# Two DFT stages of a fused GFNet and mixture-of-experts kernel: full-array products against quarter-array products of sums and differences

## The chip, the cores and the metric

The kernel runs on one core of one Trainium2 chip. The metric is device time in microseconds, from the first to the last instruction. Engine names follow the profile: PE is TensorE (matmul), PEld its weight loads, DVE is VectorE, ACT is ScalarE, POOL is GpSimd, SP is the engine that issues most transfers.

## The reference: what is computed

Two layers in a row, all in fp32. First a global filter over the sequence: a real FFT of length 2496 per batch and channel, a product with a complex filter, and the inverse. Then a top-1 mixture of experts over the 8 x 2496 = 19968 rows that come out.

```python
# batch 8, seq 2496, dim 256
X = np.fft.rfft(x, axis=1)
Y = X * (filt_r + 1j * filt_i)[None]
y = np.fft.irfft(Y, n=2496, axis=1)             # -> (19968, 256)

logits = y @ w_gate                             # 8 experts
expert_idx = np.argmax(logits, axis=1)
gate_w = softmax(logits)[row, expert_idx]
for e in range(8):                              # rows sorted by expert
    h = np.maximum(x_sorted[lo:hi] @ w1[e], 0)  # 256 -> 1024
    y_sorted[lo:hi] = h @ w2[e]                 # 1024 -> 256
out = gate_w[:, None] * y_sorted[inv_perm]
```

## The kernel before

The FFT is a product of two short DFTs: 2496 = 39 x 64, with q in 0..38 and t in 0..63. Per batch there are four stages of matmuls. Stage one (`stage_a`) takes the DFT over q (39 points, real input, so 20 frequencies f with real and imaginary part, 40 numbers). Stage two (`stage_b`) is the complex DFT over t and the filter. Stage three (`stage_c`) goes back over t. Stage four (`stage_d`) goes back over q. Between the stages the data goes through DRAM (`zd`, `ud`) to change the layout. Then each batch is routed: `turn_y` transposes the rows, `logits` multiplies by the gate, `route` finds each row's place, and rows are scattered into lists by expert, from which the expert matmuls (L796, L837, L854) read.

In stages one and four, three values of t are handled by one matmul through a block-diagonal matrix: 3 x 39 = 117 rows by 3 x 40 = 120 columns. A batch has 22 such groups, in six chunks `CH` of up to four groups (five of 4 and one of 2).

```python
NB, NG = 3, 22
TP, TK = NB * N1, NB * NS            # 117, 120

def bank():                          # one of 7 PSUM banks
    return ps.tile([P, 512], F32, tag="bank", name="bank")

def evac(o, i, n):                   # PSUM to SBUF, on DVE or ACT by a running estimate of both
    either(n, lambda: nc.vector.tensor_copy(o, i), lambda: nc.scalar.copy(out=o, in_=i))

def stage_a(b, c):
    i0, n = CH[c]
    xt = ins.pop(("x", b, c))
    zo = sb.tile([TK, 4, D], F32, tag="st", name="zo", bufs=4)
    for j in range(0, n, 2):
        p = bank()
        mm(p[:TK, :], lhsT=tas, rhs=xt[:TP, j:j + 2, :], start=True, stop=True)          # L342
        evac(zo[:, j:j + 2, :], p[:TK, :].rearrange("p (t d) -> p t d", t=2), 512)
    for r, m, v in columns(zd[b], i0, n):
        move(v, zo[:r, m])           # one transfer per chunk (two for the last)
    ...

def stage_d(b, c):
    ...
    yo = outs["o", b, c] = sb.tile([P, 4, DR], F32, tag="y", name="yo", bufs=YB)[:TP]
    for j in range(0, n, 2):
        p = bank()
        if i0 + j + 2 < NG:
            mm(p[:TP, :], lhsT=tds, rhs=ui[:TK, j:j + 2, :], start=True, stop=True)      # L401
        else:
            for i, k in enumerate((TK, NS)):                                             # L405
                mm(p[:TP, i * D:(i + 1) * D], lhsT=tds[:k, :], rhs=ui[:k, j + i, :], start=True, stop=True)
        evac(yo[:, j:j + 2, :D], p[:TP, :].rearrange("p (i d) -> p i d", i=2), 512)
```

After stage four each chunk is transposed, and the gate is applied. The gate's matmul has 32 output rows, and four of them go side by side to four strips of 32 rows of one PSUM tile:

```python
def turn_y(b, c):
    ...
                nc.tensor.transpose(                                                     # L476
                    pt[:, 2 * i + dh, :TP], yo[:, j + i, dh * P:(dh + 1) * P], ident[:TP, :TP])

def logits(b, g):
    ...
    for dh in range(DH):
        for j in js:                 # up to four
            mm(lt[j * CT:(j + 1) * CT], lhsT=wg[:, dh, :], rhs=pair[j][:, :, dh, :],     # L490
               start=(dh == 0), stop=(dh == DH - 1))
```

Each engine runs its instructions in program order. The program's order comes from a loop that keeps an estimated clock `now`, takes FFT steps from a list of slots (slot k holds stages two and three of batch k, stage one of batch k+1, stage four and routing of batch k-1), and puts expert matmuls of already routed batches in between. After the last FFT step only expert work is left.

```python
steps.append((..., lambda c=c: stage_a(k + 1, c), ("x", k + 1, c), 0.43 * CH[c][1]))     # us on PE, estimated
steps.append((at, lambda c=c: stage_d(k - 1, c), ..., 0.43 * CH[c][1]))
```

A matmul of fp32 stands in the trace as two instructions (two passes), so that one `mm` with a right side of 512 columns is two MATMUL lines.

Of the kernel before, what the change touches and what calls it, by code (L numbers as in the profile page):

```python
# [19 lines left out]
P = 128  # L20
S = 2496
D = 256
# [16 lines left out]

def token(q, t):  # L40
    return (q * N2 * pow(N2, -1, N1) + t * N1 * pow(N1, -1, N2)) % S


def coefficients():

    k = np.arange(S)
    of = np.zeros((N2, N1), int)
    of[k * pow(N1, -1, N2) % N2, k * pow(N2, -1, N1) % N1] = k
    return of[:, :NF]


def dft_tables():

    w = 2.0 * np.pi
    q = np.arange(N1)
    t = np.arange(N2)  # L60

    ta = np.zeros((NB, N1, NB, NS))
    td = np.zeros((NB, NS, NB, N1))
    for f in range(NF):
        ang = w * ((q * f) % N1) / N1
        for j in range(NB):
            ta[j, :, j, f] = np.cos(ang)
            td[j, f, j] = (2.0 if f else 1.0) / S * np.cos(ang)
            if f:
                ta[j, :, j, NF + f] = -np.sin(ang)  # L70
                td[j, NF + f, j] = -2.0 / S * np.sin(ang)

    ang = w * ((t[:, None] * t[None, :]) % N2) / N2
    c, sn = np.cos(ang), np.sin(ang)
    tb = np.block([[c, -sn], [sn, c]])
    tc = np.block([[c, sn], [-sn, c]])

    ids = np.zeros((NB, N1, NG))
    valid = np.zeros((NB, N1, NG))
    for j in range(NB):  # L80
        for i in range(len(range(j, N2, NB))):
            ids[j, :, i] = token(q, NB * i + j)
            valid[j, :, i] = 1.0


    sg = np.where(coefficients() <= S // 2, 1.0, -1.0)

    return {
        "ta": ta.reshape(TP, TK),
        "tb": tb,  # L90
        "tc": tc,
        "td": td.reshape(TK, TP),
        "sg": np.concatenate([sg[:, :NF // 2], sg[:, NF // 2:]]),
        "ids": ids.reshape(TP, NG),
        "valid": valid.reshape(TP, NG),
    }


def lay_x(x):

    out = np.zeros((x.shape[0], P, NG, D), x.dtype)
    q = np.arange(N1)
    for j in range(NB):
        for i in range(len(range(j, N2, NB))):
            out[:, j * N1:(j + 1) * N1, i] = x[:, token(q, NB * i + j)]
    return out
# [12 lines left out]
def kernel(  # L119
# [13 lines left out]
    valid: bass.AP,  # L133
    out: bass.AP,
# [47 lines left out]
    tas = cst.tile([TP, TK], F32, name="tas")  # L182
    tbs = cst.tile([P, P], F32, name="tbs")
    tcs = cst.tile([P, P], F32, name="tcs")
    tds = cst.tile([TK, TP], F32, name="tds")
    sgs = cst.tile([P, NF // 2], F32, name="sgs")
# [5 lines left out]
    tri = cst.tile([TP, TP], F32, name="tri")  # L192
    ones = cst.tile([TP, P], F32, name="ones")
    segs = {w: cst.tile([P, E * w], F32, name=f"seg{w}") for w in (8, NG % 8)}
    ids0 = cst.tile([TP, NG], F32, name="ids0")
    vld = cst.tile([TP, NG], F32, name="vld")
# [63 lines left out]
    def load_rest():  # L260
        nc.sync.dma_start(out=tds, in_=td)
        nc.vector.memset(wg, 0.0)
        nc.sync.dma_start(out=wg[:, :, :E], in_=moe_w_gate.rearrange("(i p) e -> p i e", p=P))
        nc.sync.dma_start(out=ids0, in_=ids)
        nc.sync.dma_start(out=vld, in_=valid)

    def make_constants():
        make_identity(nc, ident)
        nc.gpsimd.memset(ones, 1.0)
        nc.gpsimd.affine_select(  # L270
            out=tri, in_=ones[:, :TP], compare_op=ALU.is_gt, fill=0.0, base=0, pattern=[[1, TP]], channel_multiplier=-1
        )
        for w, seg in segs.items():
            nc.gpsimd.memset(seg, 1.0)
            nc.gpsimd.memset(seg.rearrange("p (e t) -> p e t", t=w)[:, :, 0:1], 0.0)
        nc.gpsimd.memset(cnt, 0.0)
        nc.gpsimd.iota(prow, pattern=[[0, 1]], base=0, channel_multiplier=1)
        nc.gpsimd.iota(tau_i, pattern=[[1, 64]], base=0, channel_multiplier=0)
        nc.vector.tensor_copy(tau0, tau_i)
        nc.gpsimd.iota(e_i, pattern=[[1, E]], base=0, channel_multiplier=0)  # L280
        nc.vector.tensor_scalar(em8, in0=e_i, scalar1=-float(E), scalar2=None, op0=ALU.add)
        nc.vector.tensor_scalar(eoff, in0=e_i, scalar1=float(TE), scalar2=None, op0=ALU.mult)
        nc.vector.memset(done, 0.0)
        nc.vector.memset(one, 1.0)


    def columns(ap, i0, n):
# [4 lines left out]
        if m < n:  # L292
            yield NS, slice(m, n), rows[(NG - 1) * TK:, :].rearrange("(i p) d -> p i d", p=NS)

# [29 lines left out]
    def load_z(b, c):  # L324
        f0, n = FH[c]
        zi = fin(("z", b, c))
        nc.sync.dma_start(out=zi[:HP, :n], in_=zd[b][:, f0:f0 + n, :])
        nc.sync.dma_start(out=zi[HP:, :n], in_=zd[b][:, NF + f0:NF + f0 + n, :])

    def load_u(b, c):  # L330
        i0, n = CH[c]
        ui = fin(("u", b, c))
        for r, m, v in columns(ud[b], i0, n):
            nc.sync.dma_start(out=ui[:r, m], in_=v)

    def stage_a(b, c):
        i0, n = CH[c]
        xt = ins.pop(("x", b, c))
        zo = sb.tile([TK, 4, D], F32, tag="st", name="zo", bufs=4)
        for j in range(0, n, 2):  # L340
            p = bank()
            mm(p[:TK, :], lhsT=tas, rhs=xt[:TP, j:j + 2, :], start=True, stop=True)  # L342
            evac(zo[:, j:j + 2, :], p[:TK, :].rearrange("p (t d) -> p t d", t=2), 512)
# [31 lines left out]
    def stage_c(b, f):  # L375
# [8 lines left out]
        if j == 2:  # L384
            f0 = f - 2
            move(ud[b][:, f0:f0 + 4, :], uo[:HP])
            move(ud[b][:, NF + f0:NF + f0 + 4, :], uo[HP:])
# [3 lines left out]
    def stage_d(b, c):  # L391
        if c == 0:
            lgs[b] = sb.tile([TP, NG, E], F32, tag="lg", name="lg")
# [3 lines left out]
        yo = outs["o", b, c] = sb.tile([P, 4, DR], F32, tag="y", name="yo", bufs=YB)[:TP]  # L397
        for j in range(0, n, 2):
            p = bank()
            if i0 + j + 2 < NG:  # L400
                mm(p[:TP, :], lhsT=tds, rhs=ui[:TK, j:j + 2, :], start=True, stop=True)  # L401
            else:

                for i, k in enumerate((TK, NS)):
                    mm(p[:TP, i * D:(i + 1) * D], lhsT=tds[:k, :], rhs=ui[:k, j + i, :], start=True, stop=True)  # L405
# [6 lines left out]
    def first_a(c):  # L412
# [6 lines left out]
        for j in range(0, n, 2):  # L419
            p = bank()[:, :4 * TK]  # L420
            for h in range(DH):
                for i in range(2):
                    mm(p[:, (2 * h + i) * TK:(2 * h + i + 1) * TK], lhsT=xt[:TP, j + i, h * P:(h + 1) * P], rhs=tas,
# [46 lines left out]
    def turn_y(b, c):  # L470
        yo = outs["o", b, c]
        for j in range(0, CH[c][1], 2):
            pt = bank().rearrange("p (i q) -> p i q", i=4)
            for i in range(2):
                for dh in range(DH):
                    nc.tensor.transpose(  # L476
                        pt[:, 2 * i + dh, :TP], yo[:, j + i, dh * P:(dh + 1) * P], ident[:TP, :TP]
                    )
            yt = yts[b, c, j] = sb.tile([P, 4, TP], F32, tag="yt", name="yt", bufs=4)
            evac(yt, pt[:, :, :TP], 4 * TP)  # L480

    def logits(b, g):
# [4 lines left out]
        lt = psr.tile([P, 2, E * NG], F32, tag="rk", name="lt")[:, :, :TP]  # L487
# [4 lines left out]
        ls = sb.tile([P, 2, TP], F32, tag="ls", name="ls", bufs=1)  # L492
# [3 lines left out]
    def turn_logits(b):  # L496
        g, w, ls = outs.pop(("l", b))
        n = w // CT
        pt = bank()[:TP, :2 * w].rearrange("p (i w) -> p i w", i=2)
# [8 lines left out]
    def route(b, g):  # L508
        t0 = 8 * g
        w = min(8, NG - t0)  # L510
        lg = lgs[b][:, t0:t0 + w]
        sh3 = (TP, w, E)
        she = (TP, E, w)

        def small(name, *shape, dt=F32, tag=None, rows=TP):
# [12 lines left out]
        nc.vector.tensor_tensor(oh, oh, em8[:TP, None, :].to_broadcast(sh3), op=ALU.mult)  # L528
# [4 lines left out]
        nc.vector.tensor_tensor(idx, idx, vld[:, t0:t0 + w], op=ALU.mult)  # L533
# [3 lines left out]
            oe, idx[:, None, :].to_broadcast(she), em8[:TP, :, None].to_broadcast(she), op=ALU.is_equal  # L537
# [10 lines left out]
        mm(rk[:TP, 0, :E * w], lhsT=tri, rhs=oef, start=True, stop=True)  # L548
        mm(rk[:, 1, :E * w], lhsT=ones, rhs=oef, start=True, stop=True)
        rks = sb.tile([P, 2, 8 * E], F32, tag="rks", name="rks", bufs=1)  # L550
        nc.vector.tensor_copy(rks[:TP, 0, :E * w], rk[:TP, 0, :E * w])
# [5 lines left out]
        for c, yo in enumerate(yos):  # L557
            n = min(4, w - 4 * c)
            sh8 = (TP, n, 8)
            nc.vector.tensor_scalar(  # L560
                yo.bitcast(I32)[:, :n, D:D + 8], in0=ids0[:, t0 + 4 * c:t0 + 4 * c + n, None].to_broadcast(sh8),
# [13 lines left out]
        nc.vector.tensor_tensor(posf, runf[:TP], rks[:TP, 1, :E * w], op=ALU.subtract)  # L575
        nc.vector.tensor_tensor(posf, posf, rks[:TP, 0, :E * w], op=ALU.add)
        yield 2
        bs = sb.tile([TP, E], F32, tag="bs", name="bs", bufs=1)
        nc.vector.tensor_tensor(bs, cnt[:TP], eoff[:TP], op=ALU.add)
# [6 lines left out]
        row = sb.tile([TP, 8], U32, tag="row", name="row", bufs=2)[:, :w]  # L586
        nc.vector.tensor_copy(row, rowf)  # L587
# [3 lines left out]
        for t in range(w):  # L591
            m = N1 if t0 + t == NG - 1 else TP
# [9 lines left out]
    def pad_rows():  # L602
# [6 lines left out]
        fill = pools["moe"].tile([P, DR], F32, name="fill", bufs=1)  # L609
# [6 lines left out]
    def scatter(key, at, what):  # L616
# [4 lines left out]
            in_offset=None,  # L621
        )
# [249 lines left out]
    def slot(k):  # L872
# [19 lines left out]
        if k + 1 < B:  # L892
            for c in range(nch):
                steps.append(((0.25 if k == 0 else 0.0) + 0.7 * c / nch, lambda c=c: stage_a(k + 1, c), ("x", k + 1, c), 0.43 * CH[c][1]))
        if k > 0:
            for c in range(nch + 3):
# [3 lines left out]
                if c < nch:  # L900
                    steps.append((at, lambda c=c: stage_d(k - 1, c), ("u", k - 1, c) if k > 1 else "y", 0.43 * CH[c][1]))
                if c >= 3 and c % 2:
                    steps.append((at + 0.01, lambda c=c: logits(k - 1, (c - 3) // 2), None, 0.9))
                if 1 <= c <= nch:
                    steps.append((at + 0.03, lambda c=c: turn_y(k - 1, c - 1), None, 0.22 * CH[c - 1][1]))
# [26 lines left out]
    todo = [step[2] for step in STEPS if step[2] and step[2] != "y"]  # L932
# [124 lines left out]
    with tc.manual_schedule(  # L1057
        engines={mybir.EngineType.PE, mybir.EngineType.DVE, mybir.EngineType.Activation, mybir.EngineType.SP}
    ):
        nc.sync.dma_start(out=tas, in_=ta)  # L1060
# [5 lines left out]
        while f or e:  # L1066
# [9 lines left out]
            elif f and not halt and (not f[2] or f[2] == "y" or f[2] in ins):  # L1076
# [11 lines left out]
            if not f and not sides and not late:  # L1088
                fft.close()
                tail = ctx.enter_context(tc.tile_pool(name="tail", bufs=1))  # L1090
# [39 lines left out]
```

## Time and profile before

| | |
|---|---|
| time, median of 3 | 1567.19 us (1566.37 to 1567.67) |
| span of the profiled execution | 1549.0 us |
| TensorE busy | 1500.9 us, 97% |
| VectorE busy | 746.3 us, 48% |
| ScalarE busy | 519.8 us, 34% |
| GpSimd busy | 670.6 us, 43% |
| mean granted TensorE clock | 0.991 |
| HBM traffic | 178 GB/s over the span |

Busy time of an engine is the union of its instructions' durations. For TensorE an instruction's recorded duration includes its way through the array, so consecutive instructions overlap in the record; what one costs in a dense stream is the distance from its start to the next one's start. In a line of a group, the first number after the bar is the union of the group's durations in us, the second the mean duration of one in ns, the third the idle time ahead of them.

### The profile page before, as it was taken

What the parts mean: (1) busy time and instruction counts of PE and PEld (TensorE: products, weight loads), DVE (VectorE), ACT (ScalarE), POOL (GpSimd) and SP (SyncE); (2) the same over time, 40 slices, a digit from 0 to 9 for tenths busy, and PEclk for the clock granted to TensorE, in tenths of its full rate; (3) what the DMA queues carried; (4) which work ended last, traced back from release to release, by engine and by line L of the source; (5) the groups of instructions that cost most, each with busy time, mean ns of one, the idle gap of its engine ahead of it and who ended that gap; (6) DMA issues with size and microseconds to landing.
All of it is one profiled execution on the core that took longest, in us unless ns stands there. A gap on an engine that the chain in (4) does not pass through costs nothing.

```text
span 1549.0 us, 23842 instructions
## 1 busy us (share of the span) xinstructions
PE 1500.9 (97%) x7524; PEld 1193.1 (77%) x7524; DVE 746.3 (48%) x1916; ACT 519.8 (34%) x1053; POOL 670.6 (43%) x814
## 2 busy tenths in 40 slices
PE   7998898999999999999999999999999999999998
PEld 6543454877678767878688788888888889999997
DVE  4576757434666555465755444675334333430000
ACT  4443433333333333333332333322222232224343
POOL 3222344414535445355445544573546455741111
PEclk9999999999999999999999999999999999999999
DMA  9659897885796377454744644435455433355651
GB/s 235 191 147 302 265 288 246 242 262 168 244 290 185 111 234 215 126 158 138 203 136 129 168 143 129 144 121 182 162 174 174 154 117 99 115 178 175 181 176 38
DMA packets 116160, 276.78 MB, mean 179 GB/s; under 512 B 17155, under 2 KB 58124, under 8 KB 116037
## 3 DMA queue, kind: packets, MB, share of 16 engines
q1 hardware_dynamic: 96917, 231.93, 50.3%
q0 software_dynamic: 19120, 43.33, 8.0%
q8 instruction: 63, 1.03, 0.3%
q14 instruction: 60, 0.49, 0.1%
HBM read 195.19 MB, written 80.64 MB: 178 GB/s over the span
## 4 chain that ended last, share of the span: by engine, by line
PE 77%; DMA 10%; issue 8%; DVE 4%; POOL 1%; SPq 1%; ACT 1%; POOLq 0%; ACTq 0%; DVEq 0%
PE bank L854 30%; PE bank L796 23%; DMA out_dram<-ys,idt 5%; PE bank L401 4%; PE bank L342 4%; PE bank L356 3%; PE bank L382 3%; PE bank L837 2%; PE bank L476 2%; PE bank L753 2%; DMA ud<-uo 1%; PE lt L490 1%; DMA fin<-ud 1%; DMA ht<-in_filt_dram 1%; DVE hT L800 1%
## 5 line engine op out<-in xcount | busy, mean ns | idle before, releaser
L854 PE MATMUL bank<-w2t,hT 128*128 128x256 f32 x1984 | 441.7, 380 | 0.1
L800 DVE TENSOR_TENSOR hT<-bank,hT 128x512 f32<-128x512 f32 (+1 forms) x504 | 299.6, 627 | 294.8 <-PE bank L796 190.5
L854 PEld LDWEIGHTS bank<-w2t,hT 128*128 128x128 f32 x1984 | 373.2, 190 | 63.2 <-issue 13.6
L860 POOL DMA_INDIRECT out_dram<-ys,idt x161 | 159.9, 993 | 499.8 <-ACT ys L859 247.6
L617 POOL DMA_INDIRECT rows<-yo,row x176 | 175.0, 995 | 172.5 <-DVE row L587 59.7
L804 ACT ACTIVATE hT<-hT 128x1024 f32<-128x1024 f32 (+1 forms) x144 | 133.2, 957 | 318.8 <-DVE hT L800 318.8
L859 ACT ACTIVATE ys<-bank,gts 128x256 f32<-128x256 f32 x156 | 73.8, 475 | 406.9 <-PE bank L854 352.5
L796 PE MATMUL bank<-xT,w1t 128*128 128x256 f32 (+1 forms) x864 | 190.3, 356 | 0.0
L796 PEld LDWEIGHTS bank<-xT,w1t 128*128 128x128 f32 x864 | 151.6, 190 | 21.9 <-issue 4.8
L796 PE MATMUL bank<-sums,wsum 128*128 128x256 f32 (+1 forms) x576 | 135.5, 358 | 0.0
L854 PE MATMUL bank<-w2s,hT 128*128 x592 | 132.9, 380 | 1.2 <-DVE hT L800 1.1
L837 PEld LDWEIGHTS bank<-xT,w1t 128*128 128x128 f32 x864 | 114.9, 192 | 14.2 <-issue 7.8
L837 PE MATMUL bank<-xT,w1t 128*128 128x128 f32 (+1 forms) x864 | 124.5, 299 | 0.7 <-DMA w1t<-in_moe_w_dram 0.7
L854 PEld LDWEIGHTS bank<-w2s,hT 128*128 128x128 f32 x592 | 110.2, 190 | 15.9 <-DVE hT L800 2.1
L796 PEld LDWEIGHTS bank<-sums,wsum 128*128 128x128 f32 x576 | 100.4, 190 | 19.6 <-issue 9.4
L771 POOL TENSOR_TENSOR wsum<-w1t 128x256 f32<-128x256 f32 x72 | 52.9, 734 | 108.0 <-PE bank L796 90.1
L363 DVE TENSOR_TENSOR ys<-bank,ht 128x512 f32<-128x512 f32 x80 | 54.9, 687 | 77.8 <-PE bank L356 77.2
L747 DVE COPY idt<-xg 128x4 int32<-128x4 int32 (+2 forms) x63 | 18.8, 298 | 150.2 <-DMA out_dram<-ys,idt 141.5
L401 PE MATMUL bank<-fin,tds 120*117 120x512 f32 x140 | 70.0, 622 | 12.0 <-DMA fin<-ud 10.8
L843 ACT ACTIVATE hT<-bank 128x128 f32<-128x128 f32 (+1 forms) x214 | 63.7, 301 | 53.1 <-PE bank L837 47.8
L382 PE MATMUL bank<-ys,tcs 128*128 128x512 f32 x140 | 73.0, 603 | 3.0 <-DVE ys L372 3.0
L356 PE MATMUL bank<-fin,tbs 128*128 128x512 f32 x140 | 73.2, 605 | 1.5 <-issue 1.4
(151 smaller groups left out, 1770.9 us busy)
## 6 DMA issues: line engine op xcount, KB each, us to landing
w1t<-in_moe_w_dram SPq DMA_DIRECT2D x126, 512.0 KB, 3.7
w2t<-in_moe_w_dram SPq DMA_DIRECT2D x68, 512.0 KB, 5.2
fin<-in_x_dram SPq DMA_DIRECT2D x39, 512.0 KB, 6.7
fin<-zd SPq DMA_DIRECT2D x70, 256.0 KB, 6.0
ud<-uo SPq DMA_DIRECT2D x70, 256.0 KB, 7.6
zd<-zo SPq DMA_DIRECT2D x35, 480.0 KB, 10.1
fin<-ud SPq DMA_DIRECT2D x35, 480.0 KB, 5.5
xg<-rows SPq DMA_DIRECT2D x28, 544.0 KB, 3.6
```

Of the source, the lines that this page charges most:

```text
L356: mm(p, lhsT=tbs, rhs=zi[:, j:j + 2, :], start=True, stop=True)
L382: mm(p, lhsT=tcs, rhs=ys, start=True, stop=True)
L401: mm(p[:TP, :], lhsT=tds, rhs=ui[:TK, j:j + 2, :], start=True, stop=True)
L617: sc = nc.gpsimd.indirect_dma_start(out=rowsd, out_offset=bass.IndirectOffsetOnAxis(ap=at, axis=0), in_=what, in_offset=None,)
L796: mm(q[:, v], lhsT=left[:, v * P:(v + 1) * P], rhs=right, start=True, stop=True)
L800: nc.vector.tensor_tensor(o, q, a, op=ALU.add)
L804: nc.scalar.activation(o.rearrange("p v r c -> p v (r c)"), q.rearrange("p v r c -> p v (r c)"), AF.Relu)
L837: mm(p[:, :m], lhsT=w1t[2 * i + g][:, dh, fh, v * P:(v + 1) * P], rhs=xts[i][:, dh, :m], start=(dh == 0), stop=(dh == DH - 1))
L843: lambda: nc.scalar.activation(hT, p[:, :m], AF.Relu))
L854: mm(p[:, :D], lhsT=hs[i][k % 4 // 2][:, k // 4, k % 2, j * P:(j + 1) * P], rhs=w2, start=(k == 0), stop=(k == FT - 1))
L859: lambda: nc.scalar.activation(ys, p[:, :D], AF.Copy, scale=gate))
L860: nc.gpsimd.indirect_dma_start(out=out, out_offset=bass.IndirectOffsetOnAxis(ap=idt[i].bitcast(U32)[:, j, :], axis=0), in_=ys, in_offset=None,
```

## The change

The cosine of an angle that belongs to q equals that of 39 - q, and the sine changes its sign. So stage one can be computed from the sums x[q] + x[39-q] (20 values) for the real part and from the differences (19 values) for the imaginary part, and stage four gives back an even part and an odd part whose sum and difference are the outputs at q and 39 - q. That halves the multiplications: in place of one block of 117 x 120 for three values of t there are two of at most 60 x 60, and each fits a quarter, 64 x 64, of the array. Four quarters with different row halves and column halves are addressed by four consecutive matmuls.

The new form is used in stage four for batches 3 to 7 and in stage one for batches 5 to 7. The sums and differences of the input are made on VectorE in place (`x_sums`); the host lays x out for it (q in one column, 39 - q in another, 64-row halves for two groups of three t). The outputs of stage four are joined by one copy on ScalarE and an addition and a subtraction on VectorE. The rows of a stage-four tile go from 117 to 124 (four of them gaps), and rows that stand for nothing get a place past the end of the list, which a bound on the scatter drops. Tables and lists of ids are replaced in place between batches.

The core of the diff (cuts marked):

```diff
+SUMS_A, SUMS_D = 5, 3
+TR2 = 2 * (64 - 4) + 4
...
+    def sum_columns(ap, i0, m):
+        rows = ap.rearrange("t s d -> (t s) d")
+        for k in range(2):
+            for r in range(2):
+                n = 3 * NF if i0 + 1 < NI or r == 0 else NF
+                ...
+                yield slice(at, at + n), slice(k * m, (k + 1) * m), v     # four transfers of up to 60 rows
...
     def load_u(b, c):
+        if b >= SUMS_D:
+            for r, m, v in sum_columns(ud[b], 2 * c, n // 2):
+                nc.sync.dma_start(out=ui[r, m], in_=v)
+            return
...
+    def x_sums(b, c):
+        m, xt = CH[c][1] // 2, ins["x", b, c]
+        nc.vector.tensor_tensor(xt[:, m:2 * m], xt[:, :m], xt[:, m:2 * m], op=ALU.subtract)
+        nc.vector.scalar_tensor_tensor(
+            out=xt[:, :m], in0=xt[:, :m], scalar=2.0, in1=xt[:, m:2 * m], op0=ALU.mult, op1=ALU.subtract)
...
     def stage_a(b, c):
+        if b >= SUMS_A:
+            m = n // 2
+            for k in range(2):
+                p = bank()[:, :m * D]
+                for g in range(2):
+                    o = 64 * (g ^ k)
+                    mm(p[o:o + 64], lhsT=tas[64 * g:64 * g + 64, 64 * k:64 * k + 64],
+                       rhs=xt[64 * g:64 * g + 64, k * m:(k + 1) * m, :], start=True, stop=True)
+                evac(zo[:, k * m:(k + 1) * m, :], p.rearrange("p (i d) -> p i d", i=m), m * D)
+            for r, at, v in sum_columns(zd[b], 2 * c, m):
+                move(v, zo[r, at])
...
     def stage_d(b, c):
+        if b >= SUMS_D:
+            m = n // 2
+            ps2 = [bank()[:, :m * D], bank()[:, :m * D]]
+            for k in range(2):
+                for r in range(2):
+                    g = 64 * (r ^ k)
+                    rows = 3 * NF if i0 + n < NG or r == 0 else NF
+                    mm(ps2[k][64 * r:64 * r + 64], lhsT=tds2[g:g + rows, 64 * k:64 * k + 64],
+                       rhs=ui[g:g + rows, k * m:(k + 1) * m, :], start=True, stop=True)
+            pe, po = (p[:TR2].rearrange("p (i d) -> p i d", i=m) for p in ps2)
+            low, high = yo[:, :m, :D], yo[:, m:n, :D]
+            nc.scalar.copy(out=high, in_=po)
+            nc.vector.tensor_tensor(low, pe, high, op=ALU.add)
+            nc.vector.tensor_tensor(high, pe, high, op=ALU.subtract)
...
     def scatter(key, at, what):
+            bounds_check=TR - 1,
+            oob_is_err=False,
...
+                if k + 1 >= SUMS_A:
+                    at += 0.08
+                    steps.append((at - 0.08, lambda c=c: x_sums(k + 1, c), key, 0.0))
+                steps.append((at, lambda c=c: stage_a(k + 1, c), key, (0.28 if k + 1 >= SUMS_A else 0.43) * CH[c][1]))
...
+                                  (0.28 if k > SUMS_D else 0.43) * CH[c][1]))
...
-                    steps.append((at + 0.03, lambda c=c: turn_y(k - 1, c - 1), None, 0.22 * CH[c - 1][1]))
+                    steps.append((at + 0.03, lambda c=c: turn_y(k - 1, c - 1), ("o", k - 1, c - 1) if k > SUMS_D else None, 0.22 * CH[c - 1][1]))
```

## The prediction

> **What bounds the kernel now.** I read the busy shares of the page first, then busy time in four stretches, then the waits of TensorE, then the groups of the two changed stages, and last single instructions in the timeline.
>
> The busy shares and the stretches (us, then busy time and instruction count of PE, PEld, DVE, ACT, POOL, then granted clock, DMA share, GB/s):
>
> ```profile
> PE 1500.9 (97%) x7524; PEld 1193.1 (77%) x7524; DVE 746.3 (48%) x1916; ACT 519.8 (34%) x1053; POOL 670.6 (43%) x814
> ...
> 0.00:200.00 200.00, 169.44 (x721) 95.19 (x722) 124.25 (x311) 80.89 (x161) 61.98 (x71) 0.96 0.81 229
> 200.00:320.00 120.00, 113.80 (x498) 80.34 (x497) 65.73 (x235) 43.87 (x93) 49.83 (x53) 0.97 0.83 261
> 320.00:965.00 645.00, 641.56 (x3026) 495.18 (x3025) 354.42 (x867) 215.91 (x386) 303.85 (x361) 1.00 0.59 177
> 965.00:1549.00 584.00, 576.12 (x3284) 522.39 (x3283) 201.91 (x504) 179.18 (x413) 254.93 (x330) 1.00 0.46 147
> ```
>
> TensorE is idle for 48 us of 1549, and 37 of these lie before 320 us. From 320 us to 965 us, where the FFT steps of the later batches are mixed with expert matmuls, it is idle for 3.4 us. After 965 us there is expert work alone. The changed stages lie almost all in the dense stretch. The groups by line, restricted to stretches, place them: of the 154 instructions of stage one (L342), 66 start after 258 us, which is three batches of 22; of stage four (L401), 100 start after 300 us, five batches of 20. So work taken from TensorE there shortens the program one for one, as long as no new wait appears: expert work that fills the stretch is moved up, and the expert part at the end starts earlier.
>
> What TensorE waited for, over the whole span, in total, times, longest:
>
> ```profile
> PE bank L401 <- DMA fin<-ud: 10.8, 3, 5.7
> ...
> PE lt L490 <- DVE rks L552: 3.0, 3, 1.5
> PE bank L382 <- DVE ys L372: 3.0, 2, 1.6
> ...
> PE bank L342 <- DMA fin<-in_x_dram: 0.6, 1, 0.6
> ```
>
> The largest, stage four waiting for its data, falls at 139 and 196 us, in batches that keep the old form. VectorE holds TensorE up for some 3 us a line at most.
>
> **What one changed matmul costs now, and what quarters can do.** Two pieces of the timeline (start us, us to the last recorded end, engine, line):
>
> ```profile
> 562.15 1.88 PE L342 MATMUL bank<-fin,tas 117*120 117x512 f32 x4
> 563.87 1.02 PE L356 MATMUL bank<-fin,tbs 128*128 128x512 f32 x2
> ...
> 640.24 1.46 PE L854 MATMUL bank<-w2t,hT 128*128 128x256 f32 x6
> 641.63 1.00 PE L490 MATMUL lt<-yt,wg 128*32 128x234 f32 x16
> 642.56 0.48 PE L854 MATMUL bank<-w2t,hT 128*128 128x256 f32 x1
> ```
>
> The first two lines: four instructions of 512 columns take from 562.15 to 563.87, 1.72 us, so 0.430 us each, or 0.84 ns a column. (The chain of waits has 64 instructions of 256 columns in 13.81 us, 0.216 us each, the same rate.) The last three: the gate already uses strips of the array. Sixteen instructions of 234 columns would take 16 x 234 x 0.84 ns = 3.15 us one after another. Six of L854 at 0.216 us from 640.24 on end their slots at 641.54; L854 goes on at 642.56. The block cost 1.02 us. Four strips at a time make four rounds of 0.197, together 0.79, which leaves 0.24 us (0.23 rounded up) for going into the strips and out again. So strips with right sides of their own do run side by side in this kernel, in fp32.
>
> **What the Trainium skill says.** "TensorEngine Tiling (Array Packing)", section Tiling Modes, Key Properties: tiles work independently, and a change of tiling mode drains TensorE; the 0.24 us agrees with a drain at each end. "TensorE: Matmul & The Clock Gate", section Part 3, gives measured speedups of packing, 3.07 for four row strips and 10.6 for sixteen tiles of 32 x 32; column strips are seen in this trace (3.15 against 1.02), row halves are not, nor 64 x 64. "PSUM — Partial Sum Buffer", section PSUM bank collisions: different row tiles can't write the same bank at the same time, except to other quadrants. In the diff the two matmuls into one bank have different row halves but go to different halves of its partitions, which respects that; no run here shows it yet. "VectorE: DVE Perf Modes", section on the errata, gives (N+151)/0.96 ns for an fp32 addition of two tensors, 691 ns at N = 512; the trace has 687 with one source in PSUM (L363) and 737 with both in SBUF (L372). I use the trace's.
>
> **The change part by part.**
>
> *TensorE, stages one and four.* A chunk of four groups had two matmuls, four instructions of 512 columns: 4 x 0.430 = 1.72 us. It now has four quarter matmuls, eight instructions of 512 columns (two groups of 256). If all four quarters run side by side, that is two rounds: 2 x 0.430 + 0.24 = 1.10 us. Saved: 0.62. The last chunk of a batch has two groups: it was 2 x 0.430 (stage four: 4 x 0.216), 0.86 us, and becomes 2 x 0.216 + 0.24 = 0.67, saved 0.19. A batch and stage saves 5 x 0.62 + 0.19 = 3.3 us. Five batches of stage four and three of stage one make 8 x 3.3 = 26.3 us. The drains cost 48 x 0.24 = 11.5 us, already in it; without them it would be 38.
>
> *TensorE, after stage four.* Rows go from 117 to 124. Transposes: 44 instructions x 5 batches x 7 columns x 0.84 ns = 1.3 us. Gate: 12 rounds x 5 batches x 14 columns x 0.84 ns = 0.7 us. Net of TensorE: 26.3 - 2.0 = 24.3 us.
>
> *VectorE.* The sums: 10 operations of 0.737 and two of about 0.45 (an estimate from 0.737 and the 0.27 by which half the columns shorten L800's) a batch, 8.3 us, for three batches 25 us. The joins of stage four: 10 x 0.687 + 2 x 0.420 (an addition of 256 columns from PSUM, hT<-bank 128x256 in the groups kept apart by shape) = 7.7 us a batch, for five 38.5 us. Saved: its share of the copies (the group yo<-bank on VectorE is 12.4 us for eight batches), 7.8 us. Net +56 us. From 320 to 965 us VectorE is busy for 354 of 645 us, 55%; this makes it some 63%. Beside TensorE, so nothing on the path by itself.
>
> *ScalarE.* It has the other copies of stage four (yo<-bank 117x512, 70 of 0.59 us for eight batches, so 26 us for five). Now it has one copy a chunk, 25 of 0.59 and five shorter, 17 us. Net -9.
>
> *Transfers.* The bytes stay. A batch of stage one stores with 24 transfers in place of 7, a batch of stage four loads with 24 in place of 7: 8 x 17 = 136 more issues on SP. A store of stage one takes SP 0.305 us at least and 0.358 in the median (the view of tile zo), so some 45 us of SP's time in 700. SP waits for buffers in most of its time, hence I count nothing on the path, but a load may be issued about 1 us later.
>
> *GpSimd.* The number of row scatters stays at 22 a batch. The scatter to the output, with a bound, takes 993 ns, the one to the lists, without, 995; so the bound is free.
>
> *New waits.* Transposes of stage four now wait for matmuls, a copy on ScalarE and two operations on VectorE in a row (0.59 + 2 x 0.69 = 2 us) where they waited for one copy. Stage one waits for the sums. The order in the program leaves room (transposes are taken when the estimated clock says that they have landed, sums are put 0.08 of a slot earlier, several us), but VectorE has bursts in which its queue is behind. I put 4 us of new idle time on TensorE on this, an estimate: it is about the 3.4 us of idle time that the dense stretch has, once more.
>
> Sum: 1567.2 - 24.3 + 4 = 1547. I say 1546.
>
> **Rivals.** (1) *Quarters do not run four at a time.* If the row halves took turns, a chunk would be four rounds, 4 x 0.430 + 0.24 = 1.96 us in place of 1.72, so +0.24 for all 48 chunks, with the 2 us of wider rows +14 us: about 1581. Against it: the strips of the gate, and that the diff's order goes through all four quarters in four matmuls in a row. For it: only column strips are seen here. One in ten. (2) *VectorE becomes the wait.* If each of the 48 chunks cost TensorE 0.5 us for a late sum or join, 24 us, the gain is gone: about 1567 to 1570. For it: +56 us, and expert matmuls of L796 also need VectorE to free their banks. Against it: 63% busy, and TensorE's waits for VectorE are near zero today at 55%. One in six. (3) *The earlier end of FFT steps gives more.* The drains could be shared when two quarter chunks stand side by side, worth up to 0.24 each, and the few idle us could vanish: 1538. One in six. (4) *Transfers.* Four smaller loads in place of one could make stage four wait for its data as it does at 139 and 196 us, 5 us each; but in the dense stretch no such wait is larger than 0.5 us. One in twenty; 1555.
>
> **Range and chances.** TensorE can't gain much more than 26 us plus the idle time, so the low end is 1533, above which 2% faster (1535.9) just begins: chance 0.10. Rival 2 at its middle and part of rival 1 set the high end, 1573. Slower by over 2% (above 1598.5) needs rivals 1 and 2 together: 0.05. Within 2%: 0.85.
>
> **What would show it right or wrong.** In the profile after: PE instructions of the new stage one and stage four with eight in a group, taking about 1.1 us from slot to slot, in four starts close together and then four more after 0.43 us; PE busy lower by about 24 us and DVE busy higher by about 56; the dense stretch still with few us of idle PE; the last FFT step some us earlier. Rounds of two at a time would be rival 1; "PE <- DVE" lines of over 10 us rival 2; "PE <- DMA fin<-ud" over 15 us rival 4. The prediction is wrong if TensorE's busy time falls by 20 us or more and the time doesn't, or if it doesn't fall.

## The result and the profile after

The changed kernel takes 1573.04 us (median of 4) where the kernel before takes 1566.78 us: ratio 1.0042, 95% interval 1.0022 to 1.0062. It is slower, by a little. The prediction was 1546 us.

One fact is needed for every comparison below: the time of the kernel before is not the same everywhere. It is about 1567 us in the result and again beside the runs named f below, 1562 us beside those named g, and about 1550 us beside all others, on three chips. The profile shown before is of an execution of 1550.7 us. The changed kernel took 1573 us where the kernel before takes 1567 us (ratio 1.0042), and 1571 us where it takes 1551 us (ratio 1.0135). So ratios are compared only among runs beside the same level of the kernel before, and each table row says which. Each of these chips was used in one session only, so the chip can't be told from anything else that changed between sessions.

Busy shares of the page after, and the same four stretches (the last one longer):

```profile
PE 1502.2 (96%) x7722; PEld 1178.2 (75%) x7722; DVE 797.2 (51%) x1989; ACT 516.2 (33%) x1055; POOL 709.7 (45%) x814
...
0.00:200.00 200.00, 172.76 (x726) 96.87 (x727) 124.28 (x311) 81.18 (x163) 58.95 (x65) 0.96 0.80 235
200.00:320.00 120.00, 102.40 (x455) 69.78 (x454) 64.44 (x199) 38.51 (x82) 44.77 (x49) 0.93 0.70 224
320.00:965.00 645.00, 630.45 (x3166) 471.48 (x3165) 406.27 (x973) 210.84 (x390) 335.18 (x355) 0.99 0.61 179
965.00:1572.00 607.00, 596.55 (x3380) 540.01 (x3378) 202.25 (x507) 185.68 (x422) 270.85 (x347) 1.00 0.45 145
```

The dense stretch is no longer dense. From 320 to 965 us TensorE is idle for 14.6 us instead of 3.4 (15.2 instead of 3.6 in two traces from one chip), from 200 to 320 us for 17.6 instead of 6.2, and there its clock is lower (0.93 instead of 0.97). What TensorE waited for:

```profile
PE bank L445 <- DVE fin L430: 8.4, 2, 6.4
PE bank L445 <- issue: 6.6, 3, 3.5
...
PE bank L534 <- DMA fin<-ud: 4.5, 1, 4.5
PE bank L992 <- DVE hT L938: 3.2, 4, 1.4
PE bank L495 <- DVE ys L485: 3.0, 2, 1.6
```

L445 is the first quarter matmul of stage one, L430 the second operation of its sums. The quarters themselves do what was hoped:

```profile
588.88 1.09 PE L445 MATMUL bank<-fin,tas 64*64 64x512 f32 x8 [1.68 <-ACT yo L524]
589.90 1.35 PE L992 MATMUL bank<-w2t,hT 128*128 128x256 f32 x5
```

Eight instructions of 512 columns from 588.88 to 589.90, 1.02 us, less than the 1.72 us of four in the old form: four quarters run at once. They can do so only when both of their PSUM banks are free: two quarters write one bank, the other two a second one. In a trace of the changed kernel from a chip of the 1550 us level (r_after) five of the 40 full chunks begin with two quarters alone, and the other two follow when the second bank has been read out (four times) or the data has come (once):

```profile
427.08 1.08 PE L445 MATMUL bank<-fin,tas 64*64 64x512 f32 x4
428.74 1.07 PE L445 MATMUL bank<-fin,tas 64*64 64x512 f32 x4 [0.58 <-DVE yw L478]
```

The next matmul starts at 430.45, so this chunk took 3.37 us. The five cost 5.6 us more than five slots of 1.02.

**An account of TensorE.** The page's busy time hides this saving, because an instruction's record includes its way through the array and so covers short stalls, and because the same work at half clock is longer. So for all TensorE instructions of two traces from one chip (r_before and r_after below, spans 1548.5 and 1567.2 us) I took start to next start, and called "work" of an instruction 2.5 ns plus 0.833 ns a column (dense streams show 429 ns for 512 columns and 216 for 256), a quarter of that for instructions that run four at a time. All else is "stall", half clock included:

```
us              before   after   difference
work            1452.9   1417.1     -35.8
stall, 0-200      49.8     47.9      -1.9
stall, 200-320    12.3     22.3     +10.0
stall, 320-640     7.9     33.6     +25.7
stall, 640-965     9.2     25.6     +16.4
stall, after       5.6      9.0      +3.4
```

Work fell by 36 us, as much as the prediction has without the drains (38 less 2; the tiling changes, 48 times some 0.25, 12 us, count as stall here), and the stalls ate all of it and 18 us more.

### The profile page after: what moved, and what is told of

It is laid out like the page before. It is cut to its first block, busy times and chain, and to the rows that moved or that the text cites. A ratio compares the mean times of both kernels' runs of the same rounds, so it can differ in the third digit from the quotient of the medians.

```text
span 1572.2 us, 24727 instructions
## 1 busy us (share of the span) xinstructions
PE 1502.2 (96%) x7722; PEld 1178.2 (75%) x7722; DVE 797.2 (51%) x1989; ACT 516.2 (33%) x1055; POOL 709.7 (45%) x814
## 4 chain that ended last, share of the span: by engine, by line
PE 73%; issue 9%; DMA 8%; DVE 6%; ACT 1%; POOL 1%; SPq 0%; another core or an unknown queue 0%; POOLq 0%; ACTq 0%; DVEq 0%
PE bank L992 28%; PE bank L934 21%; DMA out_dram<-ys,idt 4%; PE bank L469 4%; PE bank L495 3%; PE bank L975 3%; PE bank L519 2%; PE bank L609 2%; PE bank L455 2%; PE bank L891 2%; PE bank L534 2%; PE lt L623 1%; DVE hT L938 1%; PE bank L445 1%; DMA fin<-ud 1%
## 5 line engine op out<-in xcount | busy, mean ns | idle before, releaser
L938 DVE TENSOR_TENSOR hT<-bank,hT 128x512 f32<-128x512 f32 (+1 forms) x504 | 299.2, 627 | 322.1 <-PE bank L934 206.0
L753 POOL DMA_INDIRECT rows<-yo,row x176 | 213.4, 1212 | 223.9 <-issue 93.6
L469 PE MATMUL bank<-fin,tbs 128*128 128x512 f32 x140 | 77.4, 642 | 2.8 <-issue 2.0
L934 PE MATMUL bank<-xT,wsum 128*128 128x256 f32 (+1 forms) x288 | 67.8, 358 | 0.0
```

The source lines that it names most:

```text
L469: mm(p, lhsT=tbs, rhs=zi[:, j:j + 2, :], start=True, stop=True)
L753: sc = nc.gpsimd.indirect_dma_start(out=rowsd, out_offset=bass.IndirectOffsetOnAxis(ap=at, axis=0), in_=what, in_offset=None, bounds_check ...
L934: mm(q[:, v], lhsT=left[:, v * P:(v + 1) * P], rhs=right, start=True, stop=True)
L938: nc.vector.tensor_tensor(o, q, a, op=ALU.add)
```

## The experiments

My theory on seeing the waits was A: the sums come too late for stage one. The rivals were J (stage four's joins), S (its scatters), T (the order of the kernel before is tuned, any other costs), and later M (a change of tiling inside stage four's last chunk).

### Each stage alone, no sums, earlier sums

```diff
 e1_four_only:
-SUMS_A, SUMS_D = 5, 3
+SUMS_A, SUMS_D = 8, 3
 e2_one_only:
+SUMS_A, SUMS_D = 5, 8
 e3_no_sums: in x_sums
-        nc.vector.tensor_tensor(xt[:, m:2 * m], ..., op=ALU.subtract)
-        nc.vector.scalar_tensor_tensor(out=xt[:, :m], ..., op1=ALU.subtract)
 e4_early_sums:
-                    steps.append((at - 0.08, lambda c=c: x_sums(k + 1, c), key, 0.0))
+                    steps.append((at - 0.20, lambda c=c: x_sums(k + 1, c), key, 0.0))
```

> Stage four by quarters from batch 3 on, stage one as before in all batches. Theory A (stage one's sums in VectorE's queue make TensorE wait, and cost more than stage one's quarters save): the stall in front of stage one is gone, the time falls below the kernel before, 1553 to 1562 us, and TensorE's idle time is within 10 us of the kernel before's 48. Theory B (the joins of stage four and its wider scatters are the loss): 1568 us or more. Theory C (both lose by the mere changes of tiling mode and a busier VectorE): between, 1563 to 1568.

> Stage one by quarters from batch 5 on with its sums on VectorE, stage four as before in all batches. Theory A: slower than the kernel before, 1572 to 1582 us, with some 15 to 20 us of stalls in front of the first quarter matmul of stage one. Theory B: faster than before, 1555 to 1562 us. Theory C: 1563 to 1570.

> Both stages by quarters, but the two VectorE operations of the sums are left out (the matmuls take the loaded x as it is, so the output is not the reference's; every other operation and the program's order stay). Theory A: the stalls before stage one go, 17 us or so with their half-clock stretches, and the time is 1545 to 1556 us. Theory B: it stays at 1566 us or more.

> As the changed kernel, but the sums are put 0.20 of a slot ahead of their place instead of 0.08, stage one stays where it is. Theory A in its form that the sums come too late in the order: the stalls before stage one shrink to under 5 us, time 1553 to 1563 us. If VectorE's load is the cause and not the order, nothing moves: 1570 to 1576 us.

| run | us | kernel before | ratio, 95% interval |
|---|---|---|---|
| e1_four_only | 1565.17 | 1550.48 | 1.0106 (1.0076 to 1.0136) |
| e2_one_only | 1557.81 | 1550.48 | 1.0047 (1.0034 to 1.0060) |
| e3_no_sums | 1551.30 | 1550.48 | 1.0007 (0.9993 to 1.0021) |
| e4_early_sums | 1559.50 | 1550.48 | 1.0059 (1.0036 to 1.0082) |

e1 contradicts A as the only cause: stage four alone, without any sums, loses 15 us. e2, stage one alone with its sums, loses 7 us, as a difference what A expected (its 1572 to 1582 us stood beside 1567). e3 supports A for its part: without the sums the loss of 20 us (1571.1 us for the changed kernel beside this level, r_after below) is gone. It saved more than the 17 us of stalls that I had named, and it ended 1 us above the kernel before and not below it, so something else eats the gain that the quarters should then show. In e4 the waits for L430 are gone from the list, but a new wait takes part of their place, for the new table of stage one. SP issues its load at 245.13 us, 16 us after the last use of the old table (229.2), and the first quarter block waits for it; an earlier place for this load was not tried.

```profile
PE bank L445 <- DMA tas<-in_ta_dram: 4.3, 1, 4.3
```

Earlier sums are worth 11 or 12 us, more than half of what leaving them out is worth.

How a late sum costs more than its wait is seen in the timeline of the changed kernel on a chip of the 1550 us level (PE, DVE; stage one's first chunk of batch 5):

```profile
254.24 1.05 PE L469 MATMUL bank<-fin,tbs 128*128 128x512 f32 x2
...
255.33 0.69 DVE L476 TENSOR_TENSOR ys<-bank,ht 128x512 f32<-128x512 f32 x1 [4.58 <-PE bank L469]
256.04 0.69 DVE L477 SCALAR_TENSOR_TENSOR yw<-bank,ht 64x512 f32<-64x512 f32 x1
256.74 0.68 DVE L478 TENSOR_TENSOR yw<-bank,ht 64x512 f32<-64x512 f32 x1
...
257.46 0.99 DVE L485 TENSOR_TENSOR ys<-ys,yw 128x512 f32<-128x512 f32 x1
258.37 1.21 DVE L428 TENSOR_TENSOR fin<-fin 128x512 f32<-128x512 f32 x1
259.61 1.10 DVE L430 SCALAR_TENSOR_TENSOR fin<-fin 128x512 f32<-128x512 f32 x1
260.76 1.99 PE L445 MATMUL bank<-fin,tas 64*64 64x512 f32 x8 [5.47 <-DVE fin L430]
262.68 2.77 PE L469 MATMUL bank<-fin,tbs 128*128 128x512 f32 x4
```

The sums (L428, L430) stand in VectorE's queue behind the four filter operations of stage two, which themselves wait for TensorE. TensorE has stage one next in its own order, so it waits through all six. VectorE was idle for 4.58 us just before. In this trace five of the 18 chunks of stage one start within 0.15 us of the end of their sums, after 5.5, 3.1, 3.5, 2.0 and 1.7 us of idle TensorE, 15.8 us in all (the list of waits puts part of this under "issue" and yo). In three of the five the sums stand behind the filter operations, in one behind the joins of stage four (L525, L526), in one behind an addition for the experts (L938). After the 5.47 us here the quarter block takes 1.92 us in place of 1.02. The stretches tell why (PE to POOL busy, then clock):

```profile
254.00:257.00 3.00, 1.29 (x5) 0.41 (x3) 1.64 (x3) 0.69 (x2) 2.16 (x3) 0.99 1.04 406
257.00:264.00 7.00, 3.23 (x10) 1.11 (x11) 3.64 (x4) 1.07 (x2) 6.90 (x9) 0.53 0.98 368
264.00:274.00 10.00, 6.91 (x30) 4.01 (x30) 8.62 (x12) 2.20 (x4) 3.95 (x6) 0.99 0.68 187
```

From 257.47 us on, 2.2 us into the idle time, the trace's record of the clock has half speed for 6.8 us. The Trainium skill, "TensorE: Matmul & The Clock Gate", Part 1, names as the condition an idle window of about 3.4 us. This trace shows half clock after less. In the 3.41 us ahead of 257.47 TensorE was still busy for 1.24 us, and in those ahead of another half-clock stretch, at 745.57, for 1.37:

```profile
254.06:257.47 3.41, 1.24 (x5) 0.41 (x3) 2.08 (x4) 0.69 (x2) 2.63 (x3) 1.00 1.03 407
742.16:745.57 3.41, 1.37 (x8) 0.68 (x4) 3.19 (x12) 0.00 (x0) 0.98 (x1) 1.00 0.92 305
```

Over the whole trace half clock stands for 45.3 us, where the kernel before has 24.9 on the same chip; 20 us more at half speed lose up to 10 us of work (an estimate; some of it is idle time anyway, so 10 is the upper end).

### The two kernels on one chip, wider scatters, no joins

```diff
 e5_rows128:
-TR2 = 2 * (64 - 4) + 4
+TR2 = P
-    tds2 = cst.tile([P, P], F32, name="tds2")
+    tds2 = tds                 # (128, 128), loaded after the old form's last use
 e7_no_joins: in stage_d
-            nc.vector.tensor_tensor(low, pe, high, op=ALU.add)
-            nc.vector.tensor_tensor(high, pe, high, op=ALU.subtract)
+            nc.vector.tensor_copy(low, pe)
```

r_before and r_after are the two kernels unchanged.

> The kernel before once more, for a profile on the same chip as the next three. Every theory: the ratio to the kernel before is 1; its TensorE stalls are what the others are compared with.

> The changed kernel once more, for a profile on the same chip as the kernel before. Every theory: ratio 1.002 to 1.007. TensorE's own work (columns by the measured pace, quarters by four) 36 us lower than before, its stalls some 45 us higher.

> The changed kernel with stage-four tiles of 128 rows instead of 124 (the four more are gaps as well; the old table of stage four gives its place to the new one to make room). Theory S (the scatter of 124 rows, 1.32 us on GpSimd in place of 0.99, delays GpSimd's sums for the expert matmuls): the scatter is back at about 1.0 us, GpSimd's busy time falls by some 36 us and the ratio to the kernel before falls by 0.005 or more, to 0.995 to 0.999. Theory J (joins and sums on VectorE are the loss): the ratio stays at 1.003 to 1.007, or rises by 0.001 for wider transposes.

> The changed kernel with the joins of stage four left out: the even part is copied by VectorE and the odd part by ScalarE, as the kernel before copied, so that 30 VectorE operations are gone and the two engines don't wait for each other (the output is not the reference's). Theory J: ratio 0.990 to 0.996. Theory S: 1.001 to 1.006.

| run | us | kernel before | ratio, 95% interval |
|---|---|---|---|
| r_before | 1550.22 (one run) | 1550.99 | |
| r_after | 1571.09 | 1550.99 | 1.0135 (1.0114 to 1.0157) |
| e5_rows128 | 1568.03 | 1550.99 | 1.0102 (1.0083 to 1.0121) |
| e7_no_joins | 1565.49 | 1550.99 | 1.0083 (1.0060 to 1.0105) |

The account above is from r_before and r_after. The ratio of r_after was not the expected one: the kernel before is faster on this chip and the changed one is not. The scatters of r_after and, second, of e5 (each group is 66 of the old form and 110 of the new):

```profile
L753 POOL DMA_INDIRECT rows<-yo,row x176 | 213.6, 1214 | 212.1 <-issue 93.3
```
```profile
L753 POOL DMA_INDIRECT rows<-yo,row x176 | 176.8, 1005 | 232.9 <-issue 82.5
```

With 128 rows the scatter is back at 1.0 us and GpSimd has 37 us less to do, as S said, but the time falls by 3 us only, and the intervals overlap. S's mechanism is there; as the main cause of the loss it falls. Without joins VectorE is busy 23 us less and the time falls by 6 us: J is a small part. Both expected more.

### Whole last chunks, and the order alone

Reading the TensorE timeline of r_after block by block, I found stage four's last chunks far too long. The first three lines are r_after, the next three e8:

```profile
479.62 1.12 PE L495 MATMUL bank<-ys,tcs 128*128 128x512 f32 x2
480.72 2.36 PE L519 MATMUL bank<-fin,tds 60*64 60x256 f32 x8
483.01 1.23 PE L623 MATMUL lt<-yt,wg 128*32 128x248 f32 x15
```
```profile
924.11 0.39 PE L686 MATMUL rk<-oe,ones 124*128 124x64 f32 x2
924.43 0.66 PE L523 MATMUL bank<-fin,tds 60*64 60x256 f32 x8
925.02 1.13 PE L938 MATMUL bank<-sums,wsum 128*128 128x256 f32 x4
```

The slot is 2.29 us where the last chunk of stage one takes 0.59. Of its four quarters two have 60 rows and two only 20 (`rows = ... else NF`). The Trainium skill, "TensorEngine Tiling (Array Packing)", Tiling Modes, lists tiles of 64 and of 32 rows as different modes and says that a change of mode drains TensorE. The order 60, 20, 60, 20 would change it at each matmul. That fits the trace: the eight instructions of such a slot start 0.27 to 0.31 us apart, one after another, and all five slots take 2.29 us.

```diff
 e8_whole_last: in stage_d and load_u
-                    rows = 3 * NF if i0 + n < NG or r == 0 else NF
+                    rows = 3 * NF
+            if i0 + n == NG:                      # rows that only reach gaps: any loaded values
+                some = ud[b].rearrange("t s d -> (t s) d")[:2 * NF, None, :]
+                nc.sync.dma_start(out=ui[64 + NF:64 + 3 * NF, 0:1], in_=some)
+                nc.sync.dma_start(out=ui[NF:3 * NF, 1:2], in_=some)
 e9_whole_early: e8 and e4 together;  e10_four_whole: e8 and e1 together
 e11_order_only: in the kernel before, estimates alone
-   stage_a(k + 1, c) ... 0.43 * CH[c][1]
+   stage_a(k + 1, c) ... (0.28 if k + 1 >= 5 else 0.43) * CH[c][1]
-   stage_d(k - 1, c) ... 0.43 * CH[c][1]
+   stage_d(k - 1, c) ... (0.28 if k > 3 else 0.43) * CH[c][1]
```

> The changed kernel, but in the last chunk of stage four all four quarter matmuls have 60 rows; the 40 rows that were left out are filled with loaded rows whose products land in gaps. Theory M (a matmul of 20 rows uses another tiling of the array than one of 60, so the eight instructions of a last chunk drain TensorE in turn, 2.29 us in place of 0.6): the block takes 0.6 us in all five batches, the stalls fall by 8 us and the ratio to the kernel before falls from 1.0135 to about 1.008. If the 2.29 us have another cause, they stay.

> Whole last chunks and the sums put 0.20 of a slot ahead. Theories M and A add up: 8 us and 11 us off the changed kernel's 1571, ratio 0.999 to 1.003. If they share their cause, ratio 1.004 to 1.008.

> Stage four alone by quarters, with whole last chunks. Theory M: 8 us below the 1565 us of stage four alone, ratio 1.004 to 1.006. If M were all that stage four loses, 14 us of saved TensorE work would show: ratio 0.991 to 0.995.

> The kernel before with nothing changed but two estimates: stage one from batch 5 on and stage four from batch 3 on count 0.28 us a group in place of 0.43, as in the change, which shifts the order of FFT steps against expert matmuls. Theory T (the kernel before is tuned to its order, and any other order costs about 10 us): ratio 1.004 to 1.010. Theories A, M and J: 0.998 to 1.002.

| run | us | kernel before | ratio, 95% interval |
|---|---|---|---|
| e8_whole_last | 1566.13 | 1550.86 | 1.0104 (1.0076 to 1.0131) |
| e9_whole_early | 1558.50 | 1550.86 | 1.0043 (1.0028 to 1.0059) |
| e10_four_whole | 1558.26 | 1550.86 | 1.0044 (1.0029 to 1.0059) |
| e11_order_only | 1555.44 | 1550.86 | 1.0029 (1.0016 to 1.0043) |

M holds as far as the rows go: with 60 rows everywhere the slot is 0.59 us in three of five cases, as e8's lines show; that the drain is what the 20 rows cost is the page's reading, not tested apart. In the other two, 1.12 and 2.24 us, the quarters did not all start together. So by the slots e8 saves 6.3 of the 8.5 us that five times 1.7 would be. The time fell by 5 us from r_after, with overlapping intervals, and by 7 us from e1 to e10, where they are apart. With earlier sums (e9) only 1 us was added to what e4 had: 12.6 us off r_after in sum, not 19. In e9's trace eight chunks run two quarters ahead of the other two and cost 11.6 us beyond their slots (5.6 in r_after), which may be where part of the rest went; no run takes this apart. e11 shows T with nothing else in the way: the same work in the shifted order costs 4.6 us, half of what T expected. So part of the loss has nothing to do with quarters.

### What is left without VectorE's added work, and in the old order

```diff
 f1_no_vector: e8, e3 and e7 together;  f6_whole_no_sums: e8 and e3 together
 f3_four_order: e10 with the estimates 0.43 of the kernel before;  f4_early_order: e9 with them
 g1_before_again: the kernel before;  g2_four_order_again: f3 again
```

> Whole last chunks, and all of VectorE's added work left out: no sums ahead of stage one, and stage four's even part copied by VectorE and its odd part by ScalarE instead of joined (the output is not the reference's). Theory V (VectorE's added operations are what eats the gain): ratio 0.988 to 0.993, near the 24 us of saved TensorE work less the 5 us of shifted order. Theory T (order): 0.997 or more.

> Whole last chunks and no sums ahead of stage one, joins in place (the output is not the reference's). Against the same without whole last chunks (ratio 1.0007) 5 us less: 0.996 to 0.999. Theory V: 4 to 8 us above the run without any added VectorE work, for the joins.

> Stage four alone by quarters with whole last chunks, but with 0.43 us a group as its estimate, as in the kernel before, so that the order of the FFT steps against the expert matmuls stays near that of before. Theory T: the 5 us of the shifted order come back, ratio 0.998 to 1.002. Theory V: 1.003 to 1.006, as with the new estimate.

> Both stages by quarters, whole last chunks, sums 0.20 of a slot ahead, and 0.43 us a group as estimate in both stages. Theory T: ratio 0.998 to 1.001 (before: 1.0043 with the new estimate). Theory V: 1.002 to 1.006.

> The kernel before once more. If the chip of this call is one of those on which it takes 1567 us, the trace shows where the 17 us are: expected as stalls of TensorE at the transfers of the first 320 us. If it takes 1550 us, the trace is that of the earlier runs. Ratio 1 in either case.

> Stage four alone by quarters, whole last chunks, estimates of the kernel before: 1554 to 1558 us on any chip, so ratio 0.993 where the kernel before takes 1567 us, and 1.003 where it takes 1550 us.

| run | us | kernel before | ratio, 95% interval |
|---|---|---|---|
| f1_no_vector | 1546.49 | 1566.88 | 0.9883 (0.9858 to 0.9909) |
| f6_whole_no_sums | 1549.66 | 1566.88 | 0.9893 (0.9876 to 0.9911) |
| f3_four_order | 1556.06 | 1566.88 | 0.9935 (0.9918 to 0.9953) |
| f4_early_order | 1572.44 | 1566.88 | 1.0039 (1.0022 to 1.0056) |
| g1_before_again | 1562.13 | 1562.11 | 1.0003 (0.9988 to 1.0018) |
| g2_four_order_again | 1554.59 | 1562.11 | 0.9952 (0.9934 to 0.9971) |

Theory V says that VectorE's added operations eat the gain. Beside the f runs the kernel before takes 1567 us, as in the result, where the changed kernel has 1.0042; the changed kernel itself was not run there. Without sums and with whole last chunks the ratio is 0.9893, without joins as well 0.9883: V holds for the sums, and the joins can't be told from nothing here. With all of VectorE's added work gone, the quarters are worth 20 us at this level, near the 24 that were predicted from TensorE's work. At the level of 1550 us f1 was not run. Its 1546 us would be only some 4 us below the kernel before there, and by the same account as above its trace has 31 us more stall than r_before's, 12 of them tiling changes. So V alone does not explain that level.

For the order the two runs disagree. Stage four alone in the old order (f3, g2) is faster than the kernel before where that takes 1567 and 1562 us. Both stages in the old order with early sums (f4) are 14 us slower than the same in the new order (e9, 1558.5 us), though f4 and e9 ran on different chips and that difference is not a paired one. So T's "old order is better" isn't a rule. f3 and g2 were not run where the kernel before takes 1550 us; by medians (1555) it would not win there. g1's trace, beside r_before's, has 12 us more stall, spread from 200 us on (200 to 320 us: 17.0 against 12.3; 320 to 480: 7.5 against 3.8; 640 to 965: 12.6 against 9.1), and 40.0 us at half clock against 24.9. I expected it all before 320 us. Why the kernel before differs between sessions, and the changed one hardly did in its two, stays open. A chip alone need not be the reason: of e10's eight executions, on one chip, one took 1547.7 us and the others 1555 to 1560.

## Why the prediction was wrong, step by step

- **The quarters: right, with a wait left out.** Predicted 1.10 us a chunk; the slot is 1.02 us, and 1.11 with the delay ahead of it (0.09, from the starts on both sides). Rival 1 (row halves in turn) is false: both halves run together wherever both banks are free, and two row halves write the two halves of one bank at once (their first instructions start 13 ns apart). The chunks that waited for their second half (5.6 us in r_after) are not in the prediction.
- **The last chunk of stage four: wrong.** Predicted 0.67 us, saved 0.19; it took 2.29. I had the 20 rows in the diff before me and counted them as 60. The term is too small by 1.7 us five times, 8.5 us by slots.
- **"New waits", 4 us: the step that failed.** It came from the idle time that the dense stretch had, as if new waits would be of the size of old ones. Stalls outside the tiling changes rose by some 42 us (53.6 less 12). Leaving out the sums alone gives 19.8 us back (1571.1 to 1551.3). That is the whole loss against the kernel before at this level, and about half of the distance between the predicted gain of 21 us and the loss of 20. "The order in the program leaves room" was the belief behind it; it was read from the estimates in the code. In the trace the sums end 0.05 to 26 us ahead of their matmul, and in five of 18 chunks TensorE stood idle until they ended (15.8 us), in three of these behind filter operations that wait for TensorE too. The 3.4 us came besides from an execution of 1550.7 us, while the sum starts from 1567.2 us; the idle time of the slower executions was in no trace that was read. For the transposes after the joins the belief was right: they had slack, and the joins cost 6 us or less.
- **VectorE's load: right in size, wrong in use.** Predicted +56 us, measured +50 (746.4 to 796.8 on one chip). I argued from 63% busy against rival 2. The busy share doesn't tell whether a result is late: VectorE was idle for 4.58 us just ahead of the six operations for which TensorE waited. Rival 2, given one in six, is what happened in kind: sums come late and the gain is gone. It was to show as 0.5 us at each of 48 chunks and as a line of waits for VectorE of over 10 us; it came as a few long waits, and the largest line shows 8.4.
- **TensorE busy 24 us lower: wrong.** It fell by 5 us (1501.8 to 1496.5) on one chip, and rose by 1 from the page shown before to the one above, though its work did fall by 24 after tiling changes. Half clock and covered stalls went into the busy time.
- **GpSimd: half right.** The bound on the scatter is free (the old form with it takes 0.99 us), but 124 rows take 1.32 us for 117 rows' 0.99, +37 us of GpSimd (213.6 against 176.8), which cost some 3 us, not clear of the noise.
- **Transfers: right.** The wait for stage four's data did not grow: 4.5 us in the page above, 8.9 on the other chip.

The sum at the level of r_after, in us: -36 of work, +12 tiling changes, +19.8 sums, +5 last chunks, +4.6 order, +5.6 joins, +3 scatters, is +14; measured +20. The terms are single edits that partly overlap (e9), so 6 us or more are not accounted for. That late sums are the largest single part is shown; the division of the rest is not.

## What to carry to other kernels

When a matmul gets a new operation of another engine in front of it, the question is not how busy that engine is but what stands ahead of the operation in that engine's queue and whether that in turn waits for TensorE; look at the timeline of the slot. Give all matmuls of a packed block the same number of rows, padding with anything whose products go to gaps (2.29 us against 0.59 here), and count the PSUM banks that a block needs at once. In a tightly ordered program compare against the same order without the change (only the estimates moved): here that alone was 5 us.

## What the runs showed of the hardware that was not expected

The same 512-column operation on VectorE with all operands in SBUF took 683 ns in the median and up to 2344 ns (the view of tile fin, minimum, median, maximum):

```profile
L428 DVE TENSOR_TENSOR fin<-fin x18: 415/683/2344, 263.1 to 670.1; 128x512 f32<-128x512 f32 x15, 128x256 f32<-128x256 f32 x3
L430 DVE SCALAR_TENSOR_TENSOR fin<-fin x18: 424/692/1099, 265.5 to 670.5; 128x512 f32<-128x512 f32 x15, 128x256 f32<-128x256 f32 x3
```

In r_after's stretch from 257 to 264 us, where L428 took 1.21 us and L430 1.10, GpSimd was busy for 6.90 of 7 us. Over that whole trace 97 such operations of 512 columns stand on L428, L430 and L485. Eleven took over 0.8 us, and each of these ran at least a quarter of its time beside arithmetic on GpSimd; of the 86 others four did. Scatters on GpSimd ran beside many of the quick ones. No run takes GpSimd's arithmetic away, so the link is seen and the cause not tested. And a stall on TensorE of 5.47 us was followed by a quarter block at 1.92 us in place of 1.02: idle time can be paid once more at half clock. After a stall of 3.10 us at 269.40 us the block took 1.02.
